# A new written order for an attention block with a routed expert layer behind it, and a different pacing of the row scatters

## The chip, the cores and the metric

The kernel runs on one core of one Trainium2 chip. The metric is the device time of one execution in microseconds (us). Before the change it is 217.41 us, the median of three runs (217.0 to 218.38). The profiled execution is a separate one: it took 221.44 us, and its trace spans 219.5 us from the first to the last instruction.

The engines are TensorE (PE, with its weight loads shown apart as PEld), VectorE (DVE), ScalarE (ACT), GpSimd (POOL) and SyncE (SP, which only issues transfers here). Each takes its own instructions in the order in which the program wrote them.

## The reference

Two blocks in a row, all in float32. The first is an attention with a sketched quadratic feature map over 4 batches, 4 heads, 1088 positions and 32 numbers per head. The second routes each of the 4352 rows of 128 numbers to one of 8 experts:

```python
def phi(x):                        # r = 8, so 64 features
    a = einsum('rd,bhsd->bhsr', S1, x)
    b = einsum('rd,bhsd->bhsr', S2, x)
    return outer(a, b)             # b h s 64
kv  = einsum('bhsf,bhsd->bhfd', phi(k), v)
z   = sum(phi(k), axis=2)
x   = (phi(q) @ kv) / (phi(q) @ z + 1e-6)       # -> (4352, 128)

logits = x @ w_gate                              # 8 experts
e      = argmax(logits, axis=1)
gate   = softmax(logits)[e];  eom = sigmoid(x @ w_output_gate)[e]
out    = gate * eom * (relu(x @ w1[e]) @ w2[e])  # w1: 128x1024, w2: 1024x128
```

Every row needs only its own expert. The kernel therefore sorts rows by expert and multiplies them in tiles of 128 rows.

## The kernel before, in words

The rows are 34 chunks of 128, in nine groups of four (the last has two). All work is cut into small stages with two-letter names and a number, and the text `PLAN` at the top is the order in which they are written. No scheduler moves anything: each engine gets its share of each stage in just that order.

**Attention.** For group g, `ks` and `qs` are the sketch matmuls of k and q (L351 of the profile), `kb` and `qb` copy one factor (ACT, L359), `kp` and `qp` form the outer products on DVE (L367), `kc` adds a group into the sums of its batch (L410), `cl`, `gt`, `gs`, `gm`, `gc` close batch b and append the gate weights to it, `qt` and `qc` turn the query features (PE L421, ACT L427), `qa` is the attention matmul (L435), and `qr`, `qx`, `ql`, `qz` divide and give x and the logits (DVE).

**Routing.** The groups make seven routes: five of one group, then groups 5 and 6, then 7 and 8. For route i, `rc` chooses experts (DVE), `rp` counts places (PE L521, L522), `rs` makes slot numbers, `rg` and `rf` the factor. `rd` prepares the send on POOL, and each `sc` sends one chunk: an indirect transfer of 128 rows from `x` to `xs` in HBM, at each row's slot (L550). `mn` and `mt` make a table of full tiles after routes 2, 4 and 5 (5, 13 and 21 tiles) and the rest after the last route; `mp` sends padding.

**Tiles.** The data of this case need 37 tiles. For tile t: a load of 128 rows of `xs` into `xin` (L651, issued by SP), `tx` (PE transpose, L865), `tv` (DVE copy to `xsT`), `tu` (8 products with w1, L877), `th` (relu on ACT, `hT`), `td` (8 products with w2, L891), `ty` (ACT, scaled into `y`) and `to` (POOL, indirect transfer of the 128 results to `out`, L905). PE shows each float32 product as two records, so x592 in the page is 37 tiles of 16.

**Who asks for what.** The two halves of a tile's weights lie in three buffers in turn. `tu` of tile t asks SP for the first half of tile t+3, and `td` of tile t asks for the second half and, after it, for the rows of tile t+5:

```python
        if t + NW < end[0]:
            weights(t + NW, 1)          # NW = 3
        if NES[0] <= t + NX < end[0]:
            want(t + NX)                # NX = 5, rows of that tile
```

`want` issues loads in order as soon as the routes that fill those tiles are written and the table is made. SP is in order too: a load that waits holds back those after it. The weights of tile t+3 overwrite those of tile t, so the issue in `td` waits until that `td` is done on PE.

**Pacing.** `pace` (L681 on) holds POOL back before some scatters. While no `y` has been made it is a drain of POOL, afterwards a copy of one column of the latest `y` (L685), which waits until that `y` is there. `sc` paces before every second scatter, except at the first of a route. The plan of before has no `to` in it: results of the first ten tiles, whose `ty` stand in the plan, are all sent after it, two at each later tile, until none is left over.

Of the kernel before, what the change touches and what calls it, by code (L numbers as in the profile page):

```python
# [23 lines left out]
TS = 128  # L24
# [6 lines left out]


PLAN = """
    ks0 kb0 ks1 kp0 kb1 ks2 kp1 kc0 kb2 kc1 kp2 qs0 kc2 qs1 qb0 cl0 qp0 gt0 qb1 kc2 gs0 qp1 qt0 ks3 qc0 gm0 kb3 ks4
    gc0 kp3 bg0 qa0 kb4 kp4 kc3 qr0 qx0 kc4 qs2 ql0 qz0 qt1 qb2 rc0 qs4 qc1 qp2 rp0 rg0 qa1 qb4 rs0 rf0 qt2 qr1 cl1
    rd0 qx1 kc4 sc0 qc2 ql1 gt1 ks5 qp4 gs1 gm1 kb5 qz1 sc0 ks6 gc1 rc1 qt4 kb6 kp6 sc0 rp1 rg1 qa2 qc4 rs1 rf1 qr2
    kp5 sc0 qx2 ks8 kc5 kb8 ql2 rd1 qz2 kc6 sc1 rc2 qs3 qb3 cl2 rg2 rp2 qp3 sc1 kc6 rs2 qt3 rf2 kp8 sc1 mn2 qc3 mt2
    qs5 qa3 qb5 rd2 sc1 qs7 qr3 qp5 gt2 qb7 qx3 gs2 qs6 sc2 ql3 gm2 qb6 qp7 qt5 gc2 qa4 qz3 sc2 qp6 ks7 qc5 rc3 qs8
    sc2 kb7 qt6 qb8 qr4 kp7 rg3 rp3 qc6 rs3 sc2 kc7 rf3 qx4 kc8 cl3 ql4 rd3 gt3 qz4 sc3 gs3 qa5 rc4 gm3 qr5 qt7 gc3
    qx5 sc3 rg4 rp4 ql5 qc7 qz5 qa6 rs4 sc3 rf4 qp8 tx0 qr6 qa7 tv0 qx6 sc3 mn4 ql6 tx1 qr7 tx2 qx7 tu0 tv1 ql7 rd4  # L40
    qz7 tx3 sc4 th0 tu1 tv3 tv2 qz6 rc5 tx4 th1 td0 sc4 tv4 rg5 mt4 tu2 ty0 sc4 td1 th2 rf5 sc4 rp5 ty1 tu3 rs5 mn5 rd5 mt5
    td2 th3 sc5 tu4 ty2 sc5 td3 th4 sc5 qt8 ty3 tx5 qc8 tx6 tv5 td4 tv6 sc5 qa8 ty4 tu5 qr8 sc5 qx8 ql8 qz8 tx7 rc6
    th5 tx8 tu6 sc5 tv8 rg6 rp6 tv7 td5 rs6 th6 rf6 sc5 mn6 tx9 ty5 mt6 tu7 sc5 td6 th7 rd6 tu8 ty6 sc6 tv9 td7 th8
    sc6 tu9 ty7 sc6 tx10 th9 tx11 td8 tv11 tv10 sc6 tu10 ty8 td9 sc6 th10 tx12 ty9 tu11 tv12 sc6 td10 th11 mp6
"""
ROUTES = ((0,), (1,), (2,), (3,), (4,), (5, 6), (7, 8))
MARKS = (2, 4, 5)
# [8 lines left out]
def kernel(  # L56
# [16 lines left out]
    DM = H * D  # L73
# [9 lines left out]
    W = DM + 16  # L83
# [4 lines left out]
    consts = ctx.enter_context(tc.tile_pool(name="consts", bufs=1))  # L88
# [10 lines left out]
    def ring(pool, tag, n, shape):  # L99
        turns[tag] = [pool.tile(shape, F32, tag=f"{tag}{i}", name=f"{tag}{i}") for i in range(n)], [0]  # L100
# [28 lines left out]
    for i, x in enumerate((S1, S2)):  # L129
        own = slice(i * r, (i + 1) * r)  # L130
        if wide:
            x, dst, n = x.bitcast(I32), bits[own].rearrange("p d w -> p (d w)"), 2 * D
        else:
            dst, n = plain[own], D
# [5 lines left out]
    groups = [range(c, min(c + GRP // 128, NC)) for c in range(0, NC, GRP // 128)]  # L140
# [89 lines left out]
    routes = [range(groups[r[0]][0], groups[r[-1]][-1] + 1) for r in ROUTES]  # L230
    duo = {g: i for i, r in enumerate(ROUTES) for g in r}
    RG = max(len(rs) for rs in routes)


# [3 lines left out]
    assert 0 < NES[0] and NE <= NT  # L238
    ring(consts, "xsT", 3, [128, TS])
    ring(consts, "hT", 2, [128, FC, TS])  # L240
    ring(consts, "y", 14, [TS, DM])
    ring(consts, "xin", 20, [TS, W])
    eps = consts.tile([128, 1], F32, tag="eps")
    nc.gpsimd.memset(eps, EPS)
    fresh = {}
    for j in {len(rs) for rs in routes}:
        fresh[j] = consts.tile([128, E, j + 1], F32, tag=f"fresh{j}", name=f"fresh{j}")
        nc.gpsimd.memset(fresh[j], 1.0)
        nc.gpsimd.memset(fresh[j][:, :, 0], 0.0)
# [74 lines left out]
    def spin(n):  # L324
        ps = ps_w("ps_idle")
        for i in range(n):
            nc.tensor.matmul(ps[:, 0, :128], idle, idle, start=True, stop=True)
# [12 lines left out]
    kz, acc, xts, Ls = {}, {}, {}, {}  # L340
# [103 lines left out]
    def shared(cs, i, ps, rc):  # L444

        n = len(cs)
        at = cs[0] - routes[i][0]
        if i not in xts:
            xts[i] = xbufs[i % 4]
            Ls[i] = work.tile([128, RG, 2 * E], F32, tag="L", bufs=3, name="L")  # L450
        rc_ = rc[:, :2 * n]
        nc.vector.reciprocal(rc_, rc_)
        nc.vector.tensor_mul(xts[i][:, at:at + n, :DM].rearrange("p c (h d) -> p c h d", h=H),
                             ps[:, :2 * n, :2 * D].rearrange("p (c a) (h d) -> p c a h d", a=2, h=2),
                             rc_.rearrange("p (c a) h -> p c (a h)", a=2).unsqueeze(3).to_broadcast((128, n, H, D)))
# [15 lines left out]
    def small(name, *shape):  # L471
        return work.tile([128, *shape], F32, tag=name, bufs=3, name=name)
# [52 lines left out]
    def slots(i, oh, pp):  # L525
        n = len(routes[i])
        t10 = small("t10", E, RG)
        nc.vector.tensor_tensor(t10[:, :, :n], pp, oh[:, :, 1:], op=ALU.mult)
        sloti = work.tile([128, RG], I32, tag="sloti", bufs=4, name="sloti")
        with nc.allow_low_precision("row numbers are whole"):  # L530
            nc.vector.tensor_reduce(sloti[:, :n], t10[:, :, :n].rearrange("p e j -> p j e"), axis=AX, op=ALU.add)
        return sloti
# [109 lines left out]
    regs, xin, xTs, hTs = {}, {}, {}, {}  # L642
# [20 lines left out]
    def first_part():  # L663
        upper()
        ps = turn(0)
        lower()
        spin(1)
        spread_S(0, ps)
# [5 lines left out]
    stages, have, did = {}, {}, set()  # L674
    tabled = [-1]
    sent, left, whole = [0], [len(r) for r in routes], set()
    asked = []
    latest = [None]
    junk = consts.tile([128, 1], F32, tag="junk")

    def pace():  # L681
        if latest[0] is None:
            nc.gpsimd.drain()
        else:
            nc.gpsimd.tensor_copy(junk, latest[0][:, :1])  # L685

    def want(*tiles):

        asked.extend(tiles)
        while asked:  # L690
            k = sum(asked[0] >= n for n in NES)
            if not whole.issuperset(range((MARKS[k] if k < len(MARKS) else len(routes)) + 1)) or k > tabled[0]:
                break
            rows(asked.pop(0))
            if not asked and len(xin) == NES[0]:

                for t in range(1, NW):
                    weights(t, 0)
                    weights(t, 1)
# [81 lines left out]
    @stage  # L781
    def qx(g):
        shared(groups[g], duo[g], have["qa", g], have["qr", g])

    @stage
    def ql(g):
# [21 lines left out]

    @stage
    def rs(i):  # L810
        have["rs", i] = slots(i, have.pop(("rc", i))[0], have.pop(("rp", i)))

    @stage
    def rf(i):
# [7 lines left out]
    @stage  # L822
    def sc(i):


        if left[i] < len(routes[i]) and sent[0] % 2 == 0:
            pace()
        sent[0] += 1
        left[i] -= 1
        next(have["rd", i], None)  # L830
        if left[i] == 0:
            whole.add(i)
            want()
# [75 lines left out]
    def do(w, n):  # L909
        stages[w](n)  # L910
        did.add((w, n))

    with tc.manual_schedule():
        spin(WARM)
        first_part()
        for w, n in plan:
            do(w, n)
        def step_(t):


            for w, n in (("tx", t + 2), ("tv", t + 2), ("tu", t + 1), ("th", t + 1), ("td", t), ("ty", t)):
                if n < NT and (w, n) not in did:
                    do(w, n)
            out_of(t)

        due = []

        def out_of(t):

            due.append(t)  # L930
            if t < done:
                return
            if len(due) > 1:
                pace()
            if t > NS - 8 and t % 2 == 0:

                if len(due) == 1:
                    pace()
                nc.gpsimd.drain()
            for n in due[:2]:  # L940
                do("to", n)
            del due[:2]

        done = max(n for w, n in plan if w == "ty") + 1

        for t in range(NS - 1):
            if t == NS - 6:
                extra = nc.values_load(more[0:1, :1], min_val=0, max_val=NT - NS,
                                       skip_runtime_bounds_check_because="as many tiles as the tables hold")
            step_(t)  # L950

        def rest(t):

            if t + 1 == NT:
                return step_(t)
            kept = [dict(x) for x in (have, xin)]
            with tc.If(extra <= t + 1 - NS) as no_more:  # L957
                end[0] = t + 1
                for w in ("td", "ty", "to"):
                    do(w, t)  # L960
            for x, k in zip((have, xin), kept):
                x.clear()
                x.update(k)
            did.difference_update([("td", t), ("ty", t), ("to", t)])
            end[0] = NT
            with no_more.Else():
                step_(t)
                rest(t + 1)
        rest(NS - 1)
# [36 lines left out]
```

## Time and profile before

| | us |
|---|---|
| median of three timed runs | 217.41 |
| profiled execution, span of the trace | 219.5 |
| PE busy in it | 205.0 |
| DVE, ACT, POOL busy | 77.8, 74.4, 84.0 |
| first `tx`, first `td` on PE | 70.73, 76.79 |
| last `rp` on PE (end of the attention's and routing's PE work) | 99.82 |
| first and last result scatter | 121.8, 215.9 |

The page gives busy time as the union of an engine's records, so PE at 93% says that there is almost always a matmul in flight, not that it is at full rate. The chain that ended last is of little help here: it holds only the last result's transfer. What helps is the list of stretches (busy time of each engine in each, granted clock, DMA share) and the timeline of PE and SP in order of time, where a bracket after a row gives the idle time before it and what ended it.

### The profile page before, as it was taken

What the parts mean: (1) busy time and instruction counts of PE and PEld (TensorE: products, weight loads), DVE (VectorE), ACT (ScalarE), POOL (GpSimd) and SP (SyncE); (2) the same over time, 40 slices, a digit from 0 to 9 for tenths busy, and PEclk for the clock granted to TensorE, in tenths of its full rate; (3) what the DMA queues carried; (4) which work ended last, traced back from release to release, by engine and by line L of the source; (5) the groups of instructions that cost most, each with busy time, mean ns of one, the idle gap of its engine ahead of it and who ended that gap; (6) DMA issues with size and microseconds to landing.
All of it is one profiled execution on the core that took longest, in us unless ns stands there. A gap on an engine that the chain in (4) does not pass through costs nothing. (4 is left out here: it accounts for less than half of the span.)

```text
span 219.5 us, 6743 instructions
## 1 busy us (share of the span) xinstructions
PE 205.0 (93%) x2470; PEld 197.4 (90%) x2470; DVE 77.8 (35%) x282; ACT 74.4 (34%) x148; POOL 84.0 (38%) x159
## 2 busy tenths in 40 slices
PE   7879999699989999979999999999999999999992
PEld 6769988598878999869999999999999999999981
DVE  4452899566888985064300001010101010101000
ACT  2113154012343253332424243434343434343430
POOL 3800023534321555364054456556523131033152
PEclk9997999959999999999999999999999999999998
DMA  5999000102649487796978999999999998998311
GB/s 161 355 386 312 25 1 31 57 13 52 214 79 315 131 289 265 249 375 219 317 251 274 341 328 332 328 333 352 357 309 346 323 360 285 309 347 296 124 44 39
DMA packets 22499, 52.25 MB, mean 238 GB/s; under 512 B 3562, under 2 KB 9196, under 8 KB 22464
## 3 DMA queue, kind: packets, MB, share of 16 engines
q1 hardware_dynamic: 19888, 46.45, 63.1%
q0 software_dynamic: 2416, 5.33, 6.4%
q8 instruction: 21, 0.34, 0.7%
q14 instruction: 14, 0.11, 0.2%
q10 hardware_dynamic: 160, 0.01, 0.0%
HBM read 51.17 MB, written 5.52 MB: 258 GB/s over the span
## 5 line engine op out<-in xcount | busy, mean ns | idle before, releaser
L891 PE MATMUL kvz<-wt,hT 128*128 128x128 f32 x592 | 72.5, 276 | 0.8 <-issue 0.5
L877 PE MATMUL w<-xsT,wt 128*128 128x128 f32 x592 | 72.3, 275 | 0.0
L891 PEld LDWEIGHTS kvz<-wt,hT 128*128 128x128 f32 x592 | 69.1, 192 | 1.2 <-issue 0.7
L877 PEld LDWEIGHTS w<-xsT,wt 128*128 128x128 f32 x592 | 69.1, 192 | 0.1
L884 ACT ACTIVATE hT<-w 128x1024 f32<-128x1024 f32 x37 | 37.9, 1024 | 53.5 <-PE w L877 35.8
L905 POOL DMA_INDIRECT out_dram<-y,xin x37 | 36.1, 974 | 48.1 <-DMA wt<-in_w_dram 20.8
L870 DVE COPY xsT<-t 128x128 f32<-128x128 f32 x38 | 10.7, 290 | 98.2 <-PE t L865 91.5
L550 POOL DMA_INDIRECT xs<-x,sloti x34 | 33.9, 998 | 28.1 <-issue 25.9
L900 ACT ACTIVATE y<-kvz,xin 128x128 f32<-128x128 f32 x37 | 13.6, 368 | 34.5 <-PE kvz L891 20.0
L435 PE MATMUL w<-kz,qpT 128*64 128x98 f32 x272 | 14.2, 251 | 1.2 <-DVE lg L461 0.5
L410 PE MATMUL kvz<-vt,kp 128*64 128x65 f32 (+1 forms) x288 | 13.3, 244 | 1.5 <-issue 1.5
L435 PEld LDWEIGHTS w<-kz,qpT 128*64 128x64 f32 x272 | 11.9, 136 | 2.6 <-issue 1.4
L410 PEld LDWEIGHTS kvz<-vt,kp 128*64 128x64 f32 (+1 forms) x288 | 11.3, 154 | 2.9 <-issue 2.4
L359 ACT COPY b_sb<-t 128x128 f32<-128x128 f32 (+1 forms) x18 | 4.7, 259 | 26.8 <-PE t L351 19.0
L547 POOL TENSOR_TENSOR x<-co,ey 128x4 f32<-128x4 f32 (+2 forms) x7 | 1.5, 207 | 29.6 <-DVE co L540 23.6
L367 DVE TENSOR_TENSOR kp<-t,b_sb 128x1024 f32<-128x1024 f32 (+1 forms) x9 | 10.3, 1157 | 6.6 <-ACT b_sb L359 5.4
L685 POOL COPY junk<-y 128x1 f32<-128x1 f32 x20 | 3.8, 189 | 22.5 <-ACT y L900 21.1
L351 PE MATMUL t<-Sb,qT 128*64 128x64 f32 x272 | 10.8, 235 | 1.5 <-issue 1.5
L351 PE MATMUL t<-Sb,kT 128*64 128x64 f32 x272 | 10.2, 230 | 1.7 <-DVE kp L367 1.4
L427 ACT COPY qpT<-w 128x1024 f32<-128x1024 f32 (+1 forms) x9 | 8.7, 965 | 8.7 <-PE w L421 8.7
L367 DVE TENSOR_TENSOR qp<-t,b_sb 128x1024 f32<-128x1024 f32 (+1 forms) x9 | 10.4, 1158 | 3.4 <-ACT b_sb L359 3.4
L351 PEld LDWEIGHTS t<-Sb,kT 128*64 128x64 f32 x272 | 9.1, 142 | 2.8 <-DVE kp L367 1.7
(134 smaller groups left out, 148.0 us busy)
## 6 DMA issues: line engine op xcount, KB each, us to landing
wt<-in_w_dram SPq DMA_DIRECT2D x79, 512.0 KB
xin<-xs SPq DMA_DIRECT2D x41, 72.0 KB
vt<-in_v_dram SPq DMA_DIRECT2D x8, 260.0 KB
kT<-in_k_dram SPq DMA_DIRECT2D x8, 256.0 KB
qT<-in_q_dram SPq DMA_DIRECT2D x8, 256.0 KB
out_dram<-y,xin POOLq DMA_INDIRECT x37
xs<-x,sloti POOLq DMA_INDIRECT x34
vt<-in_v_dram SPq DMA_DIRECT2D x1, 130.0 KB
```

Of the source, the lines that this page charges most:

```text
L351: nc.tensor.matmul(ps[64 * t:64 * (t + 1), j * H:(j + 1) * H], src[:, j * 128 + 64 * t:j * 128 + 64 * (t + 1)], Sb[i], start=i == 0 and j ...
L367: nc.vector.tensor_mul(res[:, :n], bview(av, [list(av.ap[1]), list(av.ap[2]), [0, r]]), bview(bv, [list(bv.ap[1]), [0, r], list(bv.ap[2])]))
L410: nc.tensor.matmul(acc[b][64 * h:64 * (h + 1), s], kp[p0:p0 + np_, j * H + 2 * s + h].rearrange("s i j -> s (i j)"), vt[p0:p0 + np_, j, s] ...
L427: nc.scalar.copy(qpT[:, :2 * n], ps[:, :2 * n])
L435: nc.tensor.matmul(ps[64 * t:64 * (t + 1), 2 * j + s, :VG], qpT[:, 2 * j + s, 64 * t:64 * (t + 1)], kz[(c * 128 + 64 * t) // S][:, s], sta ...
L550: apart("rows", nc.gpsimd.indirect_dma_start(out=xs[:, :], out_offset=bass.IndirectOffsetOnAxis(ap=sloti[:, j:j + 1], axis=0), in_=x[:, j] ...
L870: nc.vector.tensor_copy(have["tv", t], have.pop(("tx", t)))
L877: nc.tensor.matmul(ps[:, c], wt[t % NW][0][:, c], xT, start=True, stop=True)
L884: nc.scalar.activation(have["th", t], have.pop(("tu", t)), ACTF.Relu)
L891: nc.tensor.matmul(ps, hT[:, c], wt[t % NW][1][:, c], start=(c == 0), stop=(c == FC - 1))
L900: nc.scalar.activation(have["ty", t], have.pop(("td", t)), ACTF.Copy, scale=xin[t][:, DM:DM + 1])
L905: apart("out", nc.gpsimd.indirect_dma_start(out=out, out_offset=bass.IndirectOffsetOnAxis(ap=x.bitcast(I32)[:, DM + 1:DM + 2], axis=0), in ...
```

## The change

It does four things:

1. A new text of `PLAN`. The attention stages and routes are ordered differently (a group of k earlier here, a group of q later there), the first table comes later in the plan, and 16 tiles instead of 11 are carried through to `td` in it, with `tx` up to tile 18 instead of 12.
2. Eleven `to` now stand in the plan, between the scatters of the last two routes and after them. A `to` there sends the next unsent tile, whatever its number says, and is paced like an `sc`. After the plan the list of results still to be sent leaves those out.
3. `pace`: the drain is used until the first `xin` load is written, and then a copy of `latest`, which now may also be a column of x that `qx` has just made. `sc` counts from the second scatter on, and before the first load also paces at the first scatter of a route.
4. Rings of 20 instead of 14 `y` and 26 instead of 20 `xin`, for results and rows that live longer.

The work is the same: same matmuls, same vector operations, same transfers. Only the drains and copies of pacing differ in number.

The diff, with the unchanged first and last part of the old plan left out:

```diff
-    qx5 sc3 rg4 rp4 ql5 qc7 qz5 qa6 rs4 sc3 rf4 qp8 tx0 qr6 qa7 tv0 qx6 sc3 mn4 ql6 tx1 qr7 tx2 qx7 tu0 tv1 ql7 rd4
-    qz7 tx3 sc4 th0 tu1 tv3 tv2 qz6 rc5 tx4 th1 td0 sc4 tv4 rg5 mt4 tu2 ty0 sc4 td1 th2 rf5 sc4 rp5 ty1 tu3 rs5 mn5 rd5 mt5
-    td2 th3 sc5 tu4 ty2 sc5 td3 th4 sc5 qt8 ty3 tx5 qc8 tx6 tv5 td4 tv6 sc5 qa8 ty4 tu5 qr8 sc5 qx8 ql8 qz8 tx7 rc6
-    th5 tx8 tu6 sc5 tv8 rg6 rp6 tv7 td5 rs6 th6 rf6 sc5 mn6 tx9 ty5 mt6 tu7 sc5 td6 th7 rd6 tu8 ty6 sc6 tv9 td7 th8
-    sc6 tu9 ty7 sc6 tx10 th9 tx11 td8 tv11 tv10 sc6 tu10 ty8 td9 sc6 th10 tx12 ty9 tu11 tv12 sc6 td10 th11 mp6
...
+    ks0 kb0 ks1 kp0 kb1 ks2 kp1 kc0 kb2 kc1 kp2 qs0 kc2 ks3 qb0 cl0 qp0 gt0 kb3 kc2 gs0 kp3 bg0 qt0 qs1 qc0 gm0 qb1
+    ks4 gc0 qp1 qa0 kb4 kp4 qt1 qr0 qx0 ks5 qc1 ql0 qs2 qz0 kb5 rc0 qa1 qb2 qp2 rp0 qr1 rg0 kc3 rs0 kc4 rf0 qt2 kp5
+    rd0 sc0 qc2 cl1 ks6 qx1 gt1 ql1 kb6 qs3 gs1 qz1 sc0 rc1 gm1 qb3 kc4 gc1 kc5 qp3 sc0 rg1 rp1 qa2 kp6 qt3 sc0 rs1
+    qr2 rf1 qs5 qx2 qc3 ks7 ql2 qb5 rd1 qz2 sc1 qa3 rc2 kb7 kc6 qr3 qp5 rg2 rp2 sc1 rs2 qt5 cl2 qx3 kc6 qc5 sc1 ql3
+    ks8 kp7 gt2 kb8 gs2 kp8 kc7 sc1 rf2 gm2 qz3 qs4 rc3 gc2 qa5 rd2 qb4 sc2 qp4 rp3 qr5 qs6 rs3 qx5 qt4 sc2 qb6 ql5
+    qs7 qp6 qc4 mn2 kc8 qb7 mt2 sc2 rg3 qt6 qa4 qc6 sc2 qs8 rf3 qr4 qb8 cl3 qp8 gt3 qx4 gs3 rd3 qt8 sc3 gm3 ql4 qc8
+    qz4 gc3 qa6 qp7 sc3 rc4 qt7 qr6 qc7 qx6 rp4 sc3 rg4 ql6 tx0 tx1 tv0 qa8 qz6 tx2 tv1 qr8 tu0 sc3 rs4 qx8 ql8 tv2
+    rf4 mn4 tu1 th0 mt4 rd4 sc4 td0 th1 qz8 tx3 sc4 qz5 ty0 tx4 qa7 tv3 rc5 td1 qr7 sc4 qx7 rg5 rp5 ql7 ty1 tu2 qz7
+    sc4 rc6 tu3 th2 to0 rf5 td2 tv4 th3 rs5 rd5 mn5 sc5 tu4 ty2 mt5 rg6 td3 th4 to2 rf6 rp6 ty3 tx5 sc5 rs6 tx6 td4
+    tv6 tv5 tx7 rd6 ty4 mn6 tu5 tv7 mt6 sc5 tx8 th5 tu6 sc5 td5 th6 tv8 sc5 tu7 ty5 to5 td6 th7 tx9 sc5 ty6 tx10 tu8
+    tv10 tv9 td7 sc5 th8 tu9 ty7 sc5 td8 th9 sc6 tx11 ty8 tx12 tu10 tv12 to8 td9 th10 tv11 sc6 tu11 ty9 sc6 tx13
+    th11 td10 tv13 tx14 ty10 tu12 sc6 td11 th12 tv14 to10 tx15 ty11 tu13 tv15 to11 td12 th13 sc6 tu14 ty12 sc6 td13
+    th14 to12 tx16 ty13 tx17 tv16 tu15 tv17 to13 td14 th15 to6 tx18 ty14 tu16 tv18 to14 td15 th16 to1 tu17 ty15 mp6
...
-    ring(consts, "y", 14, [TS, DM])
-    ring(consts, "xin", 20, [TS, W])
+    ring(consts, "y", 20, [TS, DM])
+    ring(consts, "xin", 26, [TS, W])
...
     def pace():
-        if latest[0] is None:
+        if not xin:
             nc.gpsimd.drain()
         else:
             nc.gpsimd.tensor_copy(junk, latest[0][:, :1])
...
     def qx(g):
         shared(groups[g], duo[g], have["qa", g], have["qr", g])
+        latest[0] = xts[duo[g]][:, groups[g][0] - routes[duo[g]][0]]
...
     def sc(i):
-        if left[i] < len(routes[i]) and sent[0] % 2 == 0:
+        if sent[0] and sent[0] % 2 == 0 and (left[i] < len(routes[i]) or not xin):
             pace()
...
         for w, n in plan:
-            do(w, n)
+            if w != "to":
+                do(w, n)
+                continue
+            if sent[0] % 2 == 0:
+                pace()
+            sent[0] += 1
+            do("to", len([n for w, n in did if w == "to"]))
...
         def out_of(t):
-            due.append(t)
+            if ("to", t) not in did:
+                due.append(t)
```

More of the change, by code (lines that the diff above doesn't have):

```diff
@@ L33 @@
 PLAN = """
[L34 to L38, printed above, removed]
@@ L39 @@
-    sc2 kb7 qt6 qb8 qr4 kp7 rg3 rp3 qc6 rs3 sc2 kc7 rf3 qx4 kc8 cl3 ql4 rd3 gt3 qz4 sc3 gs3 qa5 rc4 gm3 qr5 qt7 gc3
-    qx5 sc3 rg4 rp4 ql5 qc7 qz5 qa6 rs4 sc3 rf4 qp8 tx0 qr6 qa7 tv0 qx6 sc3 mn4 ql6 tx1 qr7 tx2 qx7 tu0 tv1 ql7 rd4
-    qz7 tx3 sc4 th0 tu1 tv3 tv2 qz6 rc5 tx4 th1 td0 sc4 tv4 rg5 mt4 tu2 ty0 sc4 td1 th2 rf5 sc4 rp5 ty1 tu3 rs5 mn5 rd5 mt5
-    td2 th3 sc5 tu4 ty2 sc5 td3 th4 sc5 qt8 ty3 tx5 qc8 tx6 tv5 td4 tv6 sc5 qa8 ty4 tu5 qr8 sc5 qx8 ql8 qz8 tx7 rc6
-    th5 tx8 tu6 sc5 tv8 rg6 rp6 tv7 td5 rs6 th6 rf6 sc5 mn6 tx9 ty5 mt6 tu7 sc5 td6 th7 rd6 tu8 ty6 sc6 tv9 td7 th8
@@ L810, in rs @@
     def rs(i):
-        have["rs", i] = slots(i, have.pop(("rc", i))[0], have.pop(("rp", i)))
+        have["rs", i] = slots(i, have["rc", i][0], have.pop(("rp", i)))
     @stage
```

## The prediction

> **What bounds the kernel now.** I read the stretches first: six windows cut where the kind of work changes.
>
> ```profile
> core 0: us, PE busy (x) PEld busy (x) DVE busy (x) ACT busy (x) POOL busy (x), PEclk, DMA share, GB/s
> 0.00:22.00 22.00, 18.31 (x339) 16.41 (x340) 9.51 (x31) 4.77 (x12) 6.56 (x53) 0.92 0.89 303
> 22.00:38.00 16.00, 16.00 (x352) 14.88 (x348) 14.06 (x42) 6.51 (x21) 3.38 (x4) 1.00 0.06 19
> 38.00:51.00 13.00, 10.84 (x160) 9.47 (x158) 7.40 (x26) 1.95 (x8) 6.37 (x10) 0.74 0.10 35
> 51.00:78.60 27.60, 25.76 (x440) 23.53 (x435) 24.16 (x82) 10.22 (x31) 9.97 (x14) 1.00 0.57 172
> 78.60:100.00 21.40, 19.47 (x180) 18.79 (x178) 9.78 (x51) 7.53 (x15) 11.33 (x18) 1.00 0.85 299
> 100.00:209.00 109.00, 109.00 (x979) 109.00 (x979) 12.55 (x53) 41.32 (x60) 42.73 (x58) 1.00 0.90 305
> ```
>
> From 100 to 209 us PE never pauses at full clock: the tiles are PE's, and no order makes them shorter. Ahead of that there are three things to win. Up to 22 us the inputs arrive at a DMA share of 0.89. From 22 to 78.6 us DVE is busy 14.06 of 16.00 and 24.16 of 27.60 us, so PE and DVE are close to one another as bounds. Between, 38 to 51 us, the clock is 0.74 and PE pauses.
>
> Second, the timeline of PE, for the pauses (the bracket is idle time before the row):
>
> ```profile
> 38.91 0.69 PE L351 MATMUL t<-Sb,kT 128*64 128x64 f32 x16 [0.69 <-DVE kp L367]
> ...
> 40.50 0.38 PE L410 MATMUL kvz<-vt,kp 128*64 128x65 f32 x4 [0.37 <-issue]
> ...
> 64.69 0.41 PE L384 MATMUL ps_kzT<-ident,kz 128*64 128x128 f32 x2 [0.62 <-DVE kz L375]
> ...
> 69.23 1.57 PE L435 MATMUL w<-kz,qpT 128*64 128x98 f32 x32 [0.52 <-DVE lg L461]
> ...
> 97.68 0.30 PE L865 MATMUL t<-ident,xin 128*128 128x128 f32 x1 [1.61 <-DVE t L504]
> ```
>
> Three waits for DVE in the attention come to 0.69 + 0.62 + 0.52 = 1.83 us. The `issue` rows (40.50 and three like it, 1.46 us in all) wait for nothing the profile shows. The last row is the transpose of tile 8. It is put down to DVE, but the only tile it reads is `xin`, so I looked at who loads that, in the timeline of SP:
>
> ```profile
> 90.11 0.33 SPq L651 DMA_DIRECT2D xin<-xs  x1
> 91.17 1.09 SPq L659 DMA_DIRECT2D wt<-in_w_dram  x2
> 92.82 0.33 SPq L651 DMA_DIRECT2D xin<-xs  x1
> 93.58 0.33 SPq L659 DMA_DIRECT2D wt<-in_w_dram  x1
> 94.46 0.33 SPq L651 DMA_DIRECT2D xin<-xs  x1
> ```
>
> The rows of tile 8 are the load at 92.82 us (the ninth of them). PE's sequencer record of the wait on that load's semaphore ends at 97.57 us, so PE waited for rows that took 4.8 us from issue to use. That is the fact my forecast rests on.
>
> **What the Trainium skill says.** "DMA: Bandwidth & Descriptors", section on queues, rings and completion order: one issuing engine owns a ring on each of the 16 DMA engines, and each ring is consumed in order. A row load is issued right behind a 512 KB half of weights, so it goes behind it. The trace agrees: at issue 110.44 us (tile 12) the first packet moves at 112.4 and the last at 114.4 us, while for tile 38, where little else is queued, issue 205.9 ends at 207.5. "TensorE: Matmul & The Clock Gate", Part 2 (what happens when you issue a matmul): only weight loads are pulled ahead, matmuls stay in program order. So a `tx` that waits holds the `tu` behind it, as at 97.68, where the `tu` at 97.82 followed at once. The same page, Part 1 (the clock gate): the clock is full or half, decided in windows of 3413 ns. The trace agrees: the record of the clock has half speed for 3.4 us from 16.1 and for 6.8 us from 43.4 us, each after a pause, whereas the 1.61 us at 96 brought none.
>
> **The change, part by part.**
>
> *Attention and routing order.* I summed PE and DVE work in plan order, with durations from the rows (sketch group 1.03 us, `qa` 1.45, `qt` 1.0, `tu` and `td` 1.8 each, `kp` 1.2, `rc` 1.75, `mt` about 3.2). For each PE stage that needs a DVE result, PE work ahead of it less DVE work up to it is its slack. Before, the slack sinks to 2.2 (`kc7`), 1.4 (`gt3`, `qa5`), 1.1 (`qa6`) and 1.0 us (`tu0`). After, it is 4 or more nearly everywhere up to `qt8`, then 1.5 (`qa8`) and 2.0 (`tu0`, `tu1`). So the three waits of 1.83 us should mostly go: I take 1.8 us of gain. The bounds are 0 (DVE is still the bound at the end of the attention, where the slacks differ by 0.5) and 5.2 (with the half clock of 43.4 to 50.2, worth 3.4 us, gone as well). I leave the latter out, since the profiled execution took 221.44 us against 217.41 timed: those 4 us of pauses may be of the profiled run alone.
>
> *Drains.* Before scatter 12 there are now five drains instead of three (at 2, 4, 6, 8 and 10 sent; before at 2, 6 and 10). With a drain the gap between scatters is about 3.1 us, without 0.30, so POOL needs 5.5 us more. In the trace it would have been free to send earlier: route 2 was held to 48.29 us by DVE. I count POOL forward from 39.4 us (route 1): scatters at 42.2, 43.5, 47.5, 48.8, then 52.8, 54.1, 58.1 and 59.4, end 60.4. Landing takes 1.9 us (57.50 to the row load at 59.40 in the trace), so rows are asked for at 62.3 instead of 59.4. How far PE will be then: in the trace it runs 10.1 us behind its summed work at the first `qa` (13.8 us of work done at 23.94) and 20.0 behind at the first `td` (58.6 at 78.6). DVE runs 15.8 us behind its own at `rf0` (14.6 at 30.4); with a slack of 1.5 us that alone puts PE 14.3 behind. `tx0` has 51.3 us of PE work ahead, so it comes at 65.6 or later. The cost is 0, hidden behind the attention's matmuls, at most 2 us if the weights of tile 1, asked for behind the rows, come late. Behind each drain stand only POOL's scatters. The later drain of route 3, with a gap of 6.6 us, goes: it was off PE's path.
>
> *Sixteen tiles in the plan.* Here is the cost. The rows of tile t are asked for in `td` of tile t-5, behind that stage's weights, once that `td` is done. In the steady part of before the written order is `td` (t-5), then `tx tu td tx tu td`, then `tx` t: 7.2 us of PE work. The new order places transposes in pairs, and each second one early. Counting in the plan, between the end of `td` t-5 and `tx` t there are: tile 8, 4.8 us (before 5.3); tile 10, `tu7 td6 tx9`, 3.8 us (before 9.4); tile 12, `tu9 td8 tx11`, 3.8 us (before 7.5); tile 14, `tu11 tx13 td10`, 3.8; tile 15, 3.8; tile 17, 3.8; tile 18, 3.9 us. What it takes: from the end of `td` to the issue 0.94 us (109.50 to 110.44), from issue to the last packet 3.4 to 4.8, mean 4.1 over tiles 12 to 20, and 0.37 until PE goes on (97.2 to 97.57). Sum 5.4 us, between 4.7 and 6.1. So `tx` 10, 12, 14 and 17 each wait 5.4 - 3.75 = 1.65 us. 15 and 18 don't, for the wait of 14 and 17 falls between their asking and their use. Tile 8 waits about 0.4. The sum is 4 x 1.65 + 0.4 = 7.0 us; before, tile 8 alone waited 1.6. The net cost is 5.4 us (2.6 to 7.8). It is not given back: behind a waiting `tx` stands all of PE, and after it PE is the bound to the end. If the transfers, freed by PE's pauses, went as for tile 38 (2.3 us from issue to use), the cost would be nil.
>
> *Results between the scatters.* A `to` is 0.97 us of POOL and 64 KB. POOL is busy 42.73 of 109 us, and nothing waits for a result but the ring of `y`, which grows to 20: cost 0, hidden beside PE. Each `to` waits for its own `y`, and the scatters behind it with it. Counted the same way, routes 5 and 6 still land before their rows are asked for, tile 13 perhaps 0.7 us late, with 5.7 + 1.65 us of PE work in hand. The larger rings cost nothing in time. The tail (last `ty`, last transfer) is the same.
>
> Sum: 217.4 - 1.8 + 5.4 = 221.0 us.
>
> **The rivals.**
> - *A, my forecast: row loads asked for too late.* 219.6 to 223.5. For it: 4.8 us measured against 3.8 in hand. Chance 0.45.
> - *B, the order of the attention and the waits cancel:* the loads are faster once PE leaves them room, say 0.9 us for each of four waits, plus 0.4, less 1.6: +2.4, less 1.8: 218.0 (215.3 to 219.5). For it: DMA share 0.85 rather than 0.90 from 78.6 to 100 us. Chance 0.23.
> - *C, faster:* loads hidden (tile 8 loses its 1.6 too), waits for DVE gone (1.8), and one spell of half clock less (1.7): 212.3, or 214 with part of it. For it: the stretch 38 to 51. Against: 4.8 us. Chance 0.20.
> - *D, slower still:* the pauses bring the half clock, as at 43.4: two windows, each 3.4 us at half speed, 3.4 us more: 224.4. Against: the 1.61 us wait did not. Chance 0.12.
>
> **Numbers.** 221.0 is A. Slower by over 1% (219.6) is A and nearly all of D: 0.55. Within 1% is B: 0.24. Faster: 0.21. For 8 in 10 the range reaches into C to 213.5 and into D to 225.
>
> **What would show it.** In the new trace: `tx` 10, 12, 14 and 17 with an idle bracket of 1 to 2 us before them on PE and none in 15 and 18; other `tx` waiting, or these not, refute the counting. The first `td` between 70 and 78 us tells what the attention's order brought; fewer and shorter waits for `kp`, `kz`, `lg`. Rows of tile 0 asked for near 62 us. I would be wrong if the loads land within 3.8 us of `td`, or if the half clock falls elsewhere.

## The result and the profile after

The changed kernel takes 226.05 us (median of four runs, 225.4 to 227.19) against 217.2 us (215.74 to 218.38): a ratio of 1.0416, 95% interval 1.0338 to 1.0495. It is slower, by 8.9 us where 3.6 were forecast, and just outside the range (213.5 to 225). Its profiled execution took 225.68 us, the trace spans 223.9. Executions more than 1.5% longer than the fastest of their kernel are left out of the ratios, here and below, but not of the medians, so the two can differ.

The stretches, cut where the prediction cut them (us, then busy time of PE, PE's weight loads, DVE, ACT and POOL, granted clock, DMA share, GB/s):

```profile
0.00:22.00 22.00, 19.30 (x372) 17.54 (x374) 10.31 (x32) 5.06 (x13) 6.53 (x53) 1.00 0.88 308
22.00:38.00 16.00, 15.85 (x348) 14.53 (x345) 14.37 (x42) 5.78 (x19) 3.77 (x5) 1.00 0.05 16
38.00:51.00 13.00, 12.56 (x281) 11.42 (x280) 11.57 (x36) 4.70 (x14) 5.95 (x10) 1.00 0.10 34
51.00:78.60 27.60, 25.73 (x349) 23.50 (x346) 23.89 (x99) 11.57 (x30) 13.68 (x21) 1.00 0.71 237
78.60:100.00 21.40, 18.84 (x165) 18.17 (x163) 9.09 (x49) 7.54 (x14) 10.23 (x16) 1.00 0.84 268
100.00:214.00 114.00, 106.72 (x933) 105.77 (x934) 8.37 (x29) 38.97 (x56) 41.35 (x57) 0.99 0.84 281
```

Two rows have changed. From 38 to 51 us the clock is full and PE busy 12.56 of 13 us, where it was 10.84 at 0.74: the first `td` starts at 69.77 us instead of 76.79. In the last row PE was busy for all 109.00 of 109 us before, and now it pauses for 7.3 us of 114. The page names the cause in one group (matmuls, busy time and mean, then idle time before them and its releaser):

```profile
L868 PE MATMUL t<-ident,xin 128*128 128x128 f32 x38 | 10.3, 284 | 9.8 <-DMA xin<-xs 9.8
```

These are the transposes, waiting for rows. The timeline of PE has them one by one; the order of the tiles is known, so each row can be named:

```profile
88.86 0.30 PE L868 MATMUL t<-ident,xin 128*128 128x128 f32 x1 [1.32 <-DMA xin<-xs]
91.69 0.33 PE L868 MATMUL t<-ident,xin 128*128 128x128 f32 x1 [0.52 <-DMA xin<-xs]
101.47 0.30 PE L868 MATMUL t<-ident,xin 128*128 128x128 f32 x1 [2.19 <-DMA xin<-xs]
101.60 3.40 PE L880 MATMUL w<-xsT,wt 128*128 128x128 f32 x16
...
111.52 0.33 PE L868 MATMUL t<-ident,xin 128*128 128x128 f32 x1 [0.87 <-DMA xin<-xs]
119.31 0.33 PE L868 MATMUL t<-ident,xin 128*128 128x128 f32 x1 [0.20 <-DMA xin<-xs]
124.85 0.30 PE L868 MATMUL t<-ident,xin 128*128 128x128 f32 x1 [1.63 <-DMA xin<-xs]
134.16 0.30 PE L868 MATMUL t<-ident,xin 128*128 128x128 f32 x1 [1.76 <-DMA xin<-xs]
154.00 0.33 PE L868 MATMUL t<-ident,xin 128*128 128x128 f32 x1 [1.34 <-DMA xin<-xs]
```

They are tiles 7, 8, 10, 12, 14, 15, 17 and 21. Behind tile 10's wait of 2.19 us the sixteen matmuls of a `tu` take 3.40 us instead of 1.95: the record of the clock has half speed from 101.8 to 105.2 us. From the first `td` to the end of the trace it is 154.1 us, before 142.7: 11.4 us more, of which 8.2 are waits for rows (9.8 less the 1.6 of before) and 1.7 the half clock (half of 3.41); the other 1.5 were not followed. The 7.0 us won ahead of the first `td` hide much of that when the traces are compared (219.5 and 223.9), but not in the times: the profiled execution of before was itself 4 us slower than the timed ones.

### The profile page after: what moved, and what is told of

The parts are those of the page before. It is cut to its first block, busy times and chain, and to the rows that moved or that the text cites. A ratio compares the mean times of both kernels' runs of the same rounds, so it can differ in the third digit from the quotient of the medians.

```text
span 223.9 us, 6744 instructions
## 1 busy us (share of the span) xinstructions
PE 203.9 (91%) x2470; PEld 195.4 (87%) x2470; DVE 77.6 (35%) x282; ACT 75.4 (34%) x148; POOL 84.4 (38%) x163
## 5 line engine op out<-in xcount | busy, mean ns | idle before, releaser
L880 PE MATMUL w<-xsT,wt 128*128 128x128 f32 x592 | 73.7, 279 | 0.0
L880 PEld LDWEIGHTS w<-xsT,wt 128*128 128x128 f32 x592 | 70.6, 196 | 0.0
L873 DVE COPY xsT<-t 128x128 f32<-128x128 f32 x38 | 10.8, 289 | 114.0 <-PE t L868 108.7
L868 PE MATMUL t<-ident,xin 128*128 128x128 f32 x38 | 10.3, 284 | 9.8 <-DMA xin<-xs 9.8
L687 POOL COPY junk<-y 128x1 f32<-128x1 f32 x23 | 4.3, 186 | 36.3 <-ACT y L903 36.3
L868 PEld LDWEIGHTS t<-ident,xin 128*128 128x128 f32 x38 | 5.4, 146 | 11.5 <-issue 7.6
L437 PE MATMUL w<-kz,qpT 128*64 128x98 f32 x272 | 13.3, 249 | 1.0 <-DVE lg L463 1.0
L353 PE MATMUL t<-Sb,kT 128*64 128x64 f32 x272 | 11.7, 247 | 1.7 <-issue 1.2
L353 PEld LDWEIGHTS t<-Sb,kT 128*64 128x64 f32 x272 | 10.4, 159 | 2.7 <-issue 1.8
L412 PE MATMUL kvz<-vt,kp 128*64 128x65 f32 (+1 forms) x288 | 10.7, 224 | 0.4 <-DVE kp L369 0.4
L412 PEld LDWEIGHTS kvz<-vt,kp 128*64 128x64 f32 (+1 forms) x288 | 9.4, 137 | 1.4 <-DVE kp L369 0.7
```

Of the source, the lines that this page charges most:

```text
L353: nc.tensor.matmul(ps[64 * t:64 * (t + 1), j * H:(j + 1) * H], src[:, j * 128 + 64 * t:j * 128 + 64 * (t + 1)], Sb[i], start=i == 0 and j ...
L412: nc.tensor.matmul(acc[b][64 * h:64 * (h + 1), s], kp[p0:p0 + np_, j * H + 2 * s + h].rearrange("s i j -> s (i j)"), vt[p0:p0 + np_, j, s] ...
L437: nc.tensor.matmul(ps[64 * t:64 * (t + 1), 2 * j + s, :VG], qpT[:, 2 * j + s, 64 * t:64 * (t + 1)], kz[(c * 128 + 64 * t) // S][:, s], sta ...
L868: nc.tensor.transpose(have["tx", t], xin[t][:, :DM], ident)
L873: nc.vector.tensor_copy(have["tv", t], have.pop(("tx", t)))
L880: nc.tensor.matmul(ps[:, c], wt[t % NW][0][:, c], xT, start=True, stop=True)
```

## The experiments

The experiments came in five sets (1 to 4, 5 to 8, 9 and 10, and two in 11). Each set ran on one chip with runs of the kernel before beside it, which took 217.2, 216.7, 216.3, 225.6 and 225.4 us. Why the last two sets are slower isn't known: the first and the last both ran on a chip numbered 8. Times of different sets are therefore compared by their ratio to the before of the set.

**1. Rows asked for eight tiles ahead, new order.** Expected:

> The changed kernel with the rows of a tile asked for 8 tiles ahead instead of 5 (the first 8 tiles at the start). Theory 1, rows asked for too late: the 9.8 us of waits of tx for xin shrink to 1.5 us or less and the spell of half clock goes with them, so 226.0 becomes 214.5 to 217. Theory 2, the transfers themselves are too slow because results, rows and weights now share the DMA engines: the wait only moves to the weights, and the time stays at 222 or above.

```diff
-NX = 5
+NX = 8
```

(Besides, the tiles that no `td` asks for any more, here 5 to 7, are put in line when the first table is made; the same in all such kernels.) Measured: 219.16 us, ratio 1.0048 (1.001 to 1.0087), between the two theories. No transpose waits for rows any more, so those waits came from asking too late. But PE now waits for weights, here in its timeline (the profiled execution took 220.94 us):

```profile
119.02 3.13 PE L882 MATMUL w<-xsT,wt 128*128 128x128 f32 x16 [1.83 <-DMA wt<-in_w_dram]
149.74 2.02 PE L896 MATMUL kvz<-wt,hT 128*128 128x128 f32 x16 [1.37 <-DMA wt<-in_w_dram]
152.97 2.02 PE L882 MATMUL w<-xsT,wt 128*128 128x128 f32 x16 [1.10 <-DMA wt<-in_w_dram]
```

and the waits of SP (total, times, longest) point to the reason:

```profile
SPq L653 <- DMA xs<-pad,pai: 3.9, 1, 3.9
SPq L653 <- DMA xs<-x,sloti: 3.4, 1, 3.4
```

A row load whose scatter hasn't landed when SP reaches it stops SP, and the weight loads behind it with it.

**2. The same in the old order,** with 26 row buffers. Expected:

> The kernel before with the rows asked for 8 tiles ahead instead of 5 (and 26 xin buffers, so that no load waits for a late result). Theory 1: only the 1.6 us before tile 8 can be won, so 215.0 to 216.5. Theory 2: no change, 216.5 to 218. The distance to the changed kernel with the same edit is what the attention's new order is worth: 0 to 3 us if the 7 us by which the first td comes earlier in the profile was partly the profiled run's own.

Measured: 213.07 us, ratio 0.9838 (0.98 to 0.9875), less than either theory said: the old order gains more than the 1.6 us of tile 8. In the trace no transpose waits for rows, and no half clock is left between the start and PE's end; the first `td` starts at 69.76 us, as early as in the new order. The granted clocks of all executions give an estimate of what half clock costs them (1 less the clock, times the span): 2.4 us in the kernel before, 0.7 here. So about half of the gain is half clock that stays away. Whether it stays away because of the earlier rows was not tested.

**3. Only the transposes moved back.** Expected:

> The changed kernel with its rows still asked for 5 ahead, but with tx of tiles 9 to 18 written in the steady pattern, one in front of each tu, instead of in pairs. Theory 1: 7.2 us lie between asking and use, the waits of tiles 10, 12, 14, 15 and 17 go (6.6 us and the half clock with its 1.7), those of 7, 8 and 21 stay (3.2): 217 to 219.5. Theory 2: no gain, 224 or above.

```diff
-... td6 th7 tx9 sc5 ty6 tx10 tu8 tv10 tv9 td7 sc5 th8 tu9 ...
+... td6 th7 sc5 ty6 tx9 tu8 tv9 td7 sc5 th8 tx10 tu9 tv10 ...
```

and so on to tile 18. Measured: 217.89 us, ratio 1.0026 (0.9973 to 1.0079), as theory 1 had it. In the trace, of an execution of 218.58 us, the waits for rows fall from 9.8 us to a third:

```profile
PE t L868 <- DMA xin<-xs: 3.2, 6, 1.4
```

**4. No results among the scatters.** Expected:

> The changed kernel without the eleven result scatters in the plan; results go out after it as in the kernel before. Theory 1: results between the rows are not the cause, 225 to 228 with the same waits. Theory 2: the result scatters delay the row loads, so without them the waits fall by half or more, 219 to 222.

Measured: 231.15 us, ratio 1.0717 (1.0613 to 1.082). Neither theory had it so slow. POOL's timeline shows the backlog (in the longest of five executions, 235.96 us): after the padding scatter at 129.67 nothing is sent for 22 us, sixteen results pile up, and the last go out after PE has finished (last matmul of the last tile about 224.9 us):

```profile
129.67 0.97 POOL L859 DMA_INDIRECT xs<-pad,pai  x1 [0.28 <-POOL pai L858]
152.81 0.18 POOL L687 COPY junk<-y 128x1 f32<-128x1 f32 x1 [22.17 <-ACT y L903]
...
227.44 0.97 POOL L908 DMA_INDIRECT out_dram<-y,xin  x1 [2.46 <-issue]
...
229.99 0.97 POOL L908 DMA_INDIRECT out_dram<-y,xin  x1 [0.30 <-issue]
```

PE's end to the trace's end is 8.8 us here and 4.5 with the results in the plan. The trace also has 11.3 us of waits for rows and more half clock (66 to 69, 103 to 107, 138 to 144). With sixteen tiles in the plan the kernel is slower without the `to` in it; why the rows were still later without them was not followed further.

**5. The reverse of 3: two early transposes in the old order.** Expected:

> The kernel before, with only the transposes of tiles 10 and 12 moved up to where the kernel after has them: right behind the w2 product of tiles 6 and 8, 3.8 us of PE work after their rows are asked for instead of 9.4 and 7.5. Theory 1 (the early transposes wait for their rows, whatever else is new): two waits of 1.5 to 2 us, so 220 to 221.5 us, up to 223 with a spell of half clock behind one of them. Theory 2 (the row loads of the kernel after are late because results and scatters are sent among them): here they land in time, 216.5 to 218.5 us.

```diff
-... td6 th7 ... tu9 ty7 sc6 tx10 th9 tx11 td8 tv11 tv10 sc6 tu10 ty8 td9 sc6 th10 tx12 ...
+... td6 tx10 th7 ... tu9 ty7 sc6 th9 tx11 td8 tx12 tv11 sc6 tu10 ty8 tv12 td9 sc6 th10 ...
```

Measured: 219.71 us, ratio 1.017 (1.0114 to 1.0226): 3.0 us more than the 216.69 beside it. The last two of these rows are tiles 10 and 12, and their 2.82 us are near the loss; the row before them is tile 8, which waits in the old order anyway (1.61 us before):

```profile
90.85 0.30 PE L865 MATMUL t<-ident,xin 128*128 128x128 f32 x1 [2.73 <-DMA xin<-xs]
100.58 0.33 PE L865 MATMUL t<-ident,xin 128*128 128x128 f32 x1 [1.49 <-DMA xin<-xs]
109.49 0.33 PE L865 MATMUL t<-ident,xin 128*128 128x128 f32 x1 [1.33 <-DMA xin<-xs]
```

**6. All obstacles out of the new order:** 3, eight tiles ahead, and `mp6` right behind the last `sc6`. Expected:

> The kernel after with all three of its row-load obstacles taken out: one transpose before each w1 product from tile 9 on, rows asked for eight tiles ahead instead of five, and the padding scatter written right after the last row scatter, so that the rows of tile 21 don't wait for it. Theory 1 (nearly the whole loss is PE waiting for rows): 213 to 215.5 us, like the kernel before with rows eight tiles ahead (213.1), no wait of a transpose for rows. Theory 2 (the new order of the attention or the scatters drawn out to 125 us cost time of their own, the latter because a row load that waits for a scatter holds up the weight loads behind it on SP): 216 to 219 us, with PE waiting for weights.

Measured: 214.31 us, ratio 0.9917 (0.9879 to 0.9955), as theory 1 had it; the waits left among the tiles are 1.5 us for weights. That is 0.8% above the old order with eight ahead (run 2).

**7. Pacing and rings alone,** the old `PLAN` in the new code. Expected:

> The pacing, the rings and the code of the kernel after with the written order of the kernel before: change 3 and 4 alone. Theory 1 (pacing costs nothing): 216 to 218.5 us, the first w2 product at 70 us (at 77 if the spell of half clock of the profile of before returns). Theory 2 (the additional drains of the first twelve scatters and the later copies hold back the rows): 219 us or more, with the first row load after 62 us and transposes of the first tiles waiting for rows.

Measured: 216.72 us, ratio 0.9961 (0.9924 to 0.9997). So pacing and rings cost nothing that can be seen; the first rows are asked for at 58.08 us.

**8. New attention, eleven tiles.** Expected:

> The kernel after with only eleven tiles in the written order instead of sixteen, no results between the scatters, and one transpose before each w1 product from tile 9 on, as in the kernel before: what is left of the change is the new order of attention and routing, the pacing and the rings. Theory 1 (the loss lies in the tiles): 216 to 218 us. Theory 2 (the new order of attention and routing is slower itself, since the kernel after with rows asked for eight tiles ahead began its sixth w2 product at 93.0 us against 90.6 us in the kernel before treated so): 219 to 221 us, the sixth w2 product 2 us or more later than 90.6 us at full clock.

Measured: 220.06 us, ratio 1.0105 (1.0061 to 1.015). The number is theory 2's, the reason isn't. This order wrote the last three `sc6` and `mp6` in a row, and SP stood before one row load, that of tile 16, for 7.4 us, until the padding landed (the load at 125.55; the one before it at 115.23):

```profile
SPq L652 <- DMA xs<-pad,pai: 7.4, 1, 7.4
```

Transposes of tiles 16 and 17 then wait 2.99 and 0.80 us and half clock follows. The sixth `td` starts at 93.12 us, with the old order at 92.97 (run 7) and 90.64 (run 2). The run doesn't tell the theories apart.

**9. A dose: six tiles ahead, in both orders.** Expected of the new order:

> The kernel after with rows asked for six tiles ahead instead of five, which puts one more tile (3.6 us of PE work) between asking and use. Theory 1 (a dose: 5.4 us are needed, 3.8 are there, with one tile more 7.4): the waits of transposes 7 to 18 go, that of tile 21, which hangs on the padding scatter, stays; 216 to 219 us. Theory 2 (rows are late because transfers and scatters crowd, so that a load takes longer when it is asked for earlier): waits of more than 4 us in sum are left, 222 us or more.

Expected of the old one:

> The kernel before with rows asked for six tiles ahead and 26 row buffers. Theory 1 (in the kernel before tile 8 alone waits for rows, 1.6 us, and one tile more covers it): 213 to 215.5 us, as with eight ahead (213.1). Theory 2 (eight ahead gained by asking for rows of tiles 5 to 7 in one go with the first ones): 215.5 to 217.5 us.

Measured: new order 215.83 us, ratio 0.9966 (0.9935 to 0.9997); old order 213.09 us, ratio 0.9842 (0.9806 to 0.9878). One tile more takes 4.5% off the new kernel. In its waits the rows have 1.6 us left, at tiles 13 and 14 (not at 21, where theory 1 left them), and weights 1.4:

```profile
PE t L870 <- DMA xin<-xs: 1.6, 2, 1.4
PE w L882 <- DMA wt<-in_w_dram: 0.8, 1, 0.8
PE kvz L896 <- DMA wt<-in_w_dram: 0.6, 1, 0.6
```

The old order is as fast as with eight ahead, so theory 1 had the number. It didn't have the reason: in the trace (an execution of 215.03 us, one of the longest of fifteen) tile 8 still waits. The wait is put down to DVE here too, but the last packet of the tile's rows moved until 90.98 us:

```profile
91.42 0.30 PE L867 MATMUL t<-ident,xin 128*128 128x128 f32 x1 [1.33 <-DVE t L504]
```

Less half clock is an estimated 0.8 us of the gain of 3.4 (granted clocks as in run 2). The larger part of it is open.

**10. The padding scatter moved,** right behind the last `sc6`: alone, and with six tiles ahead. Expected:

> The kernel after with only the padding scatter moved, rows five tiles ahead as they were. Theory 1 (tile 21 is one wait among eight, independent of the early transposes): 223.5 to 225 us, with the other waits unchanged. Theory 2 (the load blocked on SP also delays the weights behind it, and so more than one tile): under 222.5 us.

> The same with the padding scatter written right after the last row scatter. Theory 1: the wait of tile 21 goes too, another 1 to 2 us: 214.5 to 217 us, and less than after_nx6. Theory 2 (the padding scatter only moves the block of SP to an earlier place, where weights stand behind it): no less than after_nx6.

Measured: alone 227.97 us, ratio 1.0485 (1.0364 to 1.0607); with six ahead 217.15 us, ratio 1.003 (0.9992 to 1.0068). No gain in either, against theory 1 both times. Alone, tile 21 no longer waits, but tiles 10, 15 and 17 wait longer (2.88, 1.84 and 3.49 us), and the sum is 10.8 us. With six ahead its trace has 1.2 us of waits for rows and spans 212.2 us, but that is the shortest of twenty executions (213.93 us).

**11. Which part of the order?** At six ahead the new order was still 1.2% slower than the old. So it was cut at the sixth `td`, ahead of which both orders have the same tile work. Expected of the new attention with the old tiles, of the old attention with the new tiles, and of the old order with new pacing:

> Rows six tiles ahead, pacing and rings of the kernel after; written order of the kernel after up to the sixth w2 product, and from there on that of the kernel before (eleven tiles, no results between scatters, padding after the eleventh). Theory A (the 2.7 us lie in the tiles and their drawn-out scatters): 212.5 to 214 us, like the kernel before with rows six ahead (213.1). Theory B (the new order of the attention is itself slower): 215 to 216.5 us. The forecast's own step, a gain of 1.8 us from this order: 211 to 212 us.

> The reverse: the written order of the kernel before up to the sixth w2 product, and from there on the sixteen tiles, the results between scatters and the late padding of the kernel after; rows six ahead, pacing of the kernel after. Theory A: 215 to 216.5 us, with PE waiting some 3 us for rows and weights between 105 and 155 us. Theory B: 212.5 to 214 us.

> The written order of the kernel before in the code of the kernel after, with rows six ahead: pacing and rings alone. Theories A and B: 212.5 to 214 us. If it is the pacing that costs the 2.7 us: 215 us or more.

Measured, where before takes 225.58 us: 218.72 us, ratio 0.973 (0.9675 to 0.9784); 226.58 us, 0.9883 (0.981 to 0.9956); 221.98 us, 0.9893 (0.9829 to 0.9957). In ratios the new attention gains 1.6%, which neither A nor B expected. The new tiles, behind the old attention, cost nothing in ratios (0.9883 against 0.9893), but that ratio rests on three executions: all eight go from 221.96 to 230.97 us, and their median is 4.6 us above that of the old order. Since before was slower than in the other sets, three orders were run once more, side by side. Expected:

> The same kernel as nx6_new_attention (new attention, old tiles, rows six ahead), beside the two others of this call. Theory A (the attention's order gains where the old one falls into half clock between 43 and 51 us, and never costs; the tiles of the new order cost): the fastest of the three, a ratio to before of 0.97 to 0.985. Theory B (the attention's order costs, and the last call was a matter of its chip): slower than the whole old order by 1% or more.

> The same kernel as after_nx6 (whole new order, rows six ahead). Theory A: 1 to 1.5% slower than pair_new_attention, the cost of its tiles with their late scatters. Theory B: as fast as pair_new_attention.

> The same kernel as before_nx6 (whole old order, old pacing, rows six ahead). Theory A: between 0.98 and 0.99 of before, no faster than pair_new_attention. Theory B: the fastest of the three.

Measured beside 225.35 us: 219.66 us, ratio 0.9735 (0.9665 to 0.9804); 221.86 us, 0.9847 (0.9784 to 0.9911); 222.09 us, 0.9823 (0.9739 to 0.9906). The order of the three is theory A's: the new tiles cost about 1.1% (0.9847 against 0.9735, 2.5 us), and the new attention gains, by 0.9% here and 1.6% before, with intervals of almost that size. A's reason isn't shown. It let the attention gain where the old order falls into half clock between 43 and 51 us, but here the trace of the old order has no half clock between 20 us and PE's end.

How the new tiles can cost time at six ahead is seen in the trace of the whole new order (224.66 us, the longest of six). The padding goes out at 136.38 us; SP reaches the row load of tile 21 at 138.9 and waits for the landing, as its waits say:

```profile
SPq L653 <- DMA xs<-pad,pai: 7.3, 1, 7.3
```

Its timeline shows the hole between the load before and that row load:

```profile
135.69 2.54 SPq L661 DMA_DIRECT2D wt<-in_w_dram  x3
146.21 0.33 SPq L653 DMA_DIRECT2D xin<-xs  x1
```

Weights that would have been asked for in the hole come late, and PE waits for tile 21's rows and then twice for weights, 4.0 us in all. Its timeline:

```profile
148.10 0.33 PE L870 MATMUL t<-ident,xin 128*128 128x128 f32 x1 [1.09 <-DMA xin<-xs]
151.01 2.02 PE L896 MATMUL kvz<-wt,hT 128*128 128x128 f32 x16 [0.79 <-DMA wt<-in_w_dram]
155.23 2.58 PE L882 MATMUL w<-xsT,wt 128*128 128x128 f32 x16 [2.09 <-DMA wt<-in_w_dram]
```

That is shown for this trace, which has a spell of half clock (156.5 to 159.9 us) behind the last wait. That it is the 1.1% is not: run 10 moved the padding forward, and gained nothing.

**The fastest:** where before takes 225 us, the new attention with the old tiles and rows six ahead (218.72 and 219.66 us, 0.973); where it takes 217 us that order was not run, and the old order with six or eight ahead is the fastest (213.1 us, 0.984). Both beat the kernel before and the one after.

## Why the prediction was right in direction and too small

*Rows (the step "Here is the cost"): right mechanism, its term too small.* It said 7.0 us of waits, less 1.6, net 5.4. The trace has 9.8, less 1.6, net 8.2. The named tiles 8, 10, 12, 14 and 17 were to wait 7.0 us and wait 5.54. The single ones were not as counted (2.19, 0.87 and 0.20 us for tiles 10, 12 and 14, which the counting made alike), since the load needed between 3.3 us (tile 14) and 5.4 us (tile 10) from the end of `td` to its last packet. What was missing are three tiles. Tile 15 was to be covered by 14's wait, but 14 hardly waited, and 15's own load was issued 2.1 us after its `td` instead of 0.94: 1.63 us. Tile 7's load, at 83.5 us, was issued 2.2 us after its `td`: 1.32 us. The 0.94 us was tile 12's alone; over tiles 12 to 20 of the trace of before this step took 0.94 to 1.75 us. Tile 21 has nothing to do with early transposes, its load was behind the padding: 1.34 us. The 2.3 us of tile 38 count from the end of its `td`; from its issue to its last packet it took 1.6. Runs 3 and 5 show the mechanism in both directions.

*Half clock (rival D): it came.* D was argued down with the 1.61 us wait of before that brought none. Tile 10's 2.19 us did, for 1.7 us, and the three other executions have lower granted clocks (0.981 to 0.987 against 0.992), so more of it. In the trace the result is A with one of D's two windows, without the gain of the attention.

*Attention (gain of 1.8 us by three waits): this step failed.* The waits stayed: `kp` 0.44, `kz` 0.38, `qp` 0.43 and `lg` 1.03 us in the new order, 2.3 us against 1.83. Counting the slack of each stage didn't show which stage DVE would deliver late. The first `td` was early as announced (69.77 us, within 70 to 78 but for 0.2), yet the old order reaches 69.76 when its half clock at 43 us stays away (run 2), and with eight ahead the sixth `td` starts at 90.87 us in the new order (run 6) and 90.64 in the old. Where before takes 225 us the order is worth 0.9 to 1.6%, about the forecast's size or twice it, and not by those waits. With no half clock there in either trace, PE is busy 11.3 us of the stretch 38 to 51 in the new order and 10.0 in the old one (`pair_new_attention`, `pair_both_old`).

*Drains: cost 0, right* (run 7); rows were asked for at 58.9 us, not at 62.3, since POOL came through its scatters faster than counted.

*Results between the scatters: cost 0; this step failed by what it left out.* Run 4 shows that the kernel is slower without them; what they themselves cost was not measured. The step looked at routes 5 and 6 and not at the padding, which the longer plan sends at 140.84 us, and not at SP, which stops for it. The new tiles cost about 1.1% at six ahead in one comparison and nothing in another (run 11).

*The sum.* The forecast was 5.4 for late rows and -1.8 for the rest, 3.6 us. The four kernels at five and six ahead split the measured loss in the same two. One tile of lead takes 4.5% off the new order (1.0416 less 0.9966) and 1.6% off the old: net 2.9%, 6.3 us of 217. The rest is 2.7 us (0.9966 less 0.9842), 9.0 together. So the net for late rows was off by 0.9 us, and the rest by 4.5. That the net is so near is partly luck: the new order lost more by late rows than forecast, 9.8 us with some 2 us of half clock (estimated as in run 2), and the old order gained 3.4 where 1.6 was to be taken off, for reasons that run 9 leaves open. Of the 4.5 us, 1.8 is a gain of the attention that doesn't show beside an old order without half clock. The other 2.7 are a cost of the new order that was set at nothing, and its place is open: the new tiles' 2.5 us are about that size, but were measured where before takes 225 us, and there the whole new order at six ahead is only 0.2% slower than the old one (0.9847 and 0.9823). Each ratio is uncertain by 0.3 to 0.9%.

## What to carry to other kernels

For every transfer whose place in the order changes, count the work between asking for data and using it, and put the measured latency under load beside it with its spread, not its mean: in this new order one more tile of lead was worth 4.5%, more than any part of the reordering. A load that waits for a scatter holds every load behind it on its queue, so a scatter sent late must be traced to who is queued behind its reader. Cut a reordering in parts and try the parts: this one held one large loss, and smaller parts of both signs near the edge of what could be measured.

## What the runs showed of the hardware beside that

- *Waits and half clock.* Of PE's waits after the first `td`, those of 1.83, 2.09, 2.19, 2.86, 2.88, 2.99, 3.17 and 3.49 us were followed or overlapped by 3.4 us or more of half clock; 1.84, 1.97 and 2.73 us were not, nor any shorter one. The Trainium skill, "TensorE: Matmul & The Clock Gate", Part 1 (the clock gate), has the decision in windows of 3413 ns that run on regardless of the kernel. The traces agree: the spells before PE's end last 3.41 or 6.83 us, and the full clock between two spells lasts whole multiples of 3.413 us (92.16 us in the kernel after is 27 of them, 167.25 us before is 49). If the traces are cut at that grid, PE's pauses in the window just ahead of a spell come to 1.83 to 3.03 us, and in no other window after the first `td` to more than 1.84. The waits of 1.97 and 2.73 us lay across a boundary and left at most 1.71 and 1.41 us in one window. Ahead of the first `td`, among shorter matmuls, less was enough: spells at 65.15, 65.35 and 65.90 us (runs 1, 3 and 4) stand behind windows with 1.09, 0.90 and 1.21 us of pauses, though 1.36 us in another (`nx6_old_plan`) brought none.
- *Pauses without a wait.* Where before takes 225 us, PE pauses in the stretches of short matmuls with nothing waited for that the profile shows. Two rows of PE's timeline in the old order, six tiles ahead (`pair_both_old`):

```profile
38.94 0.36 PE L410 MATMUL kvz<-vt,kp 128*64 128x65 f32 x5 [0.41 <-issue]
...
49.24 0.39 PE L435 MATMUL w<-kz,qpT 128*64 128x98 f32 x4 [0.41 <-issue]
```

  From 20 us to the first `td` such pauses (of 0.15 us or more) come to 1.4 to 3.9 us in the three traces with the old attention and to 0.6 to 1.5 us in the three with the new one. In the thirteen traces of the sets where before takes 217 us they come to 0.3 us at most. The first profile of before has 2.0 us of them, four of 0.37 us just ahead of its half clock at 43 us. That they brought it, or that the new attention gains because it has fewer, was not tested.
